# Keys placed into a ring of tile slots, and the probabilities of 18 tiles multiplied on GpSimd

## The chip, the core and the metric

One core of a Trainium2 chip runs the kernel. The metric is the time of one execution in device microseconds. The engines are named as in the profile: PE (TensorE), PEld (its weight loads), DVE (VectorE), ACT (ScalarE), POOL (GpSimd) and SP (SyncE, whose queue issues every DMA here). Each engine works through its own queue in program order and waits on semaphores of the others.

## The reference

Three stages follow one another: a sparse attention, a mixture of eight experts, and a two-layer network with a rational activation. The change touches the first alone.

```
def _attn_ref(q, k, v):                  # 2 batches, 8 heads, 768 positions, 64 wide
    k_sum = k.reshape(B, H, nb, 32, D).max(axis=3)
    v_sum = v.reshape(B, H, nb, 32, D).mean(axis=3)
    scores_l = scale * q @ k.T           # kept where |i - j| < 16, else -1e9
    scores_s = scale * q @ k_sum.T + log(32)
    a = softmax(concatenate([scores_l, scores_s]))
    return a @ concatenate([v, v_sum])
def reference(...):
    x = _attn_ref(...).transpose(0, 2, 1, 3).reshape(1536, 512)
    x = _moe_ref(x, ...)     # logits, 8 rounds of row and column scaling, sum of P[:, e] * relu(x @ w1[e]) @ w2[e]
    return _moe2_ref(x, ...) # g(x @ w_in) @ w_out, g a ratio of polynomials
```

## The kernel before

The attention works on 24 tiles of 64 queries, twelve for each batch. A query tile sees 96 keys (its own 64 and 16 on each side) and 24 block maxima, so its scores have CO = 120 columns for each head; the 8 heads lie in four pairs, which makes a tile of probabilities 128 x 480.

Keys come in three loads of 256 positions for each batch. Of each load the even and odd tokens are copied apart (`by_token`, L399), transposed on PE (`transpose8`, L347) and placed into a tile `kT` of 256 positions (`place`, L359, on ACT, or the second half on DVE). `block_keys` (L375) makes the block maxima `ks` on DVE. `window` (L489) then copies for each tile the 96 keys out of one or two `kT` tiles, and the 24 block maxima, into one of three buffers `kw`; these copies are `pcopy` (L331), that is POOL instructions of line L332.

The loop of L728 sets the order of all engines. Its step s writes the scores of tile s (`scores`, L506: PE, the mask addition L526 and the negated maximum L530 on DVE), the product with the values of tile s-3 (`av`, L558), the transposition of the probabilities of tile s-2 (`trans`, L546), the normalization of tile s-1 (`norm`, L540: an addition L542, a reciprocal L543 and a multiplication L544, all on DVE), the exponentials of tile s (`exps`, L533, ACT) and the window of tile s+2. Then follows what `todo` holds for the step: token copies and placing of later keys and queries, the split of the first expert weights into a high part on POOL (`high_w1`, L135) and a low part on DVE (`low_w1`, L142), the sums of the values and their split (`sum_v`, `means_split`), and the copies of the block means into the three value buffers `vx` (`block_values`, L555, for tiles 0 to 2 of each batch). Between these stand the matmuls of the first expert unit (`mains`, L712), let in by a running credit, and through step 5 short runs of matmuls on the identity (`spin`, L424).

The scores have one PSUM buffer of their own (tag `sc`), so the scores of tile s+1 start only when the mask addition of tile s has read it; the products with the values share one in the same way (tag `xo`); the transposes of keys, queries and probabilities take turns in two (tag `tr`).

Of the kernel before, what the change touches and what calls it, by code (L numbers as in the profile page):

```python
# [10 lines left out]
F32 = mybir.dt.float32  # L11
F32R = mybir.dt.float32r
# [10 lines left out]
def kernel(  # L23
# [285 lines left out]
    with ExitStack() as actx:  # L309
# [1 line left out]
        a1 = actx.enter_context(tc.tile_pool(name="att1", bufs=1, side="right"))  # L311
        psa = actx.enter_context(tc.tile_pool(name="psa", bufs=1, space=PSUM))

        kw = [a1.tile([P, NP, CO], F32, name=f"kw{i}") for i in range(2)]
        kw.append(acc[9][:, 0:NP * CO].rearrange("p (c n) -> p c n", c=NP))
        vx = [a1.tile([CO, DM], F32, name=f"vx{i}") for i in range(3)]
        qs = [a1.tile([P, NP, LT], F32, name=f"qs{i}") for i in range(2)]
        wavg = a1.tile([P, 2 * NB], F32, name="wavg")
        wavgr = a1.tile([P, 2 * NB], F32R, name="wavgr")
        masks = [a1.tile([P, 1, CO], F32, name=f"mask{i}") for i in range(3)]  # L320
        zpad = a1.tile([P, NP, WIN], F32, name="zpad")

        nat = {}
        kT = {}
# [9 lines left out]
        def load_nat(src, nm, b, i):  # L334

            if nm == "q" and b == 0 and i < 2:
                if i:
                    t = spool.tile([P, KC, 2 * P], F32, tag="stg", name="q_0_1")
                else:
                    t = apool.tile([P, NP, LT], F32, tag="kT", name="q_0_0", bufs=4)  # L340
                t = t.rearrange("p c (h t d) -> p (c h) t d", h=2, t=2)
            else:
                t = apool.tile([P, H, 2, D], F32, tag="nat", name=f"{nm}_{b}_{i}", bufs=3)
            nc.sync.dma_start(t, src[b, :, i * LT:(i + 1) * LT, :].rearrange("h (p t) d -> p h t d", t=2))
            nat[nm, b, i] = t
# [12 lines left out]

        def place(dst, par, ps, mul, early=False):  # L359

            o = dst.rearrange("p c (n t) -> p c n t", t=2)[:, :, :, par]
            if par and not early:
                nc.vector.tensor_scalar_mul(o, ps, mul)
            else:
                nc.scalar.mul(o, ps, mul)

        def new_k(b, i):
            kT[b, i] = apool.tile([P, NP, LT], F32, tag="kT", name=f"kT_{b}_{i}", bufs=4)
            if i == 0:
                ks[b] = apool.tile([P, NP, NB], F32, tag="ks", name=f"ks_{b}")  # L370

# [3 lines left out]
        def block_keys(b, i):  # L375
            nb = LT // BLK
            nc.vector.tensor_reduce(
                out=ks[b][:, :, i * nb:(i + 1) * nb],
                in_=kT[b, i].rearrange("p c (n s) -> p c n s", s=BLK),
                axis=AX.X, op=ALU.max,  # L380
            )

        def last_keys(pss):

            nb = LT // BLK
            o = ks[0][:, :, NB - nb:NB]
            m = a1.tile([P, NP, nb], F32, name="odd")
            for dst, ps in zip((o, m), pss):
                nc.vector.tensor_reduce(
                    out=dst, in_=ps.rearrange("p c (n s) -> p c n s", s=BLK // 2), axis=AX.X, op=ALU.max  # L390
                )
            nc.vector.tensor_max(kw[0][:, :, CO - nb:CO], o, m)
            nc.vector.tensor_max(o, o, m)

        qscale = 1.0 / math.sqrt(D)
# [59 lines left out]
        def means_split(i):  # L455
            x = nat.pop(("vsum", 1, i)).rearrange("p h d -> p (h d)")
            if i < 2:
                y = spool.tile([P, KC, 2 * P], F32R, tag="stg", name=f"vhl_{i}").rearrange("p (a b) f -> p a (b f)", a=2)
            else:
                y = apool.tile([P, NP, LT], F32R, tag="kT", name="vhl_2", bufs=4).rearrange("p (a b) f -> p a (b f)", a=2)  # L460
            nc.scalar.copy(y[:, 0], x)
            nc.gpsimd.tensor_sub(y[:, 1], x, y[:, 0].bitcast(F32))
            means[i] = (y[:, 0], y[:, 1])
# [22 lines left out]
                v[b, :, c0:c1, :].rearrange("h p d -> p h d"),  # L486
            )

        def window(t, part=0):  # L489

            b, r = divmod(t, QB)
            w = kw[t % 3]
            i = r // TPL
            e = WIN
            lo, hi = (r % TPL) * QT - e, (r % TPL) * QT + QT + e
            c0, c1 = max(lo, 0), min(hi, LT)
            if part != 2 and lo < 0:
                pcopy(w[:, :, 0:e], kT[b, i - 1][:, :, LT - e:LT] if i else zpad[:, :, 0:e])
            if part != 2:
                pcopy(w[:, :, c0 - lo:c1 - lo], kT[b, i][:, :, c0:c1])  # L500
            if part != 2 and hi > LT:
                pcopy(w[:, :, WK - e:WK], kT[b, i + 1][:, :, 0:e] if i < NL - 1 else zpad[:, :, 0:e])
            if part != 1:
                pcopy(w[:, :, SO:CO], ks[b])

        def scores(t):  # L506
            b, r = divmod(t, QB)
            qt = qT[b, r // TPL]
            ps = psa.tile([P, 2, NP, P], F32, tag="sc", name=f"sc_{t}")
            w = kw[t % 3]  # L510
            i = 0 if r == 0 else (2 if r == QB - 1 else 1)
            m = masks[i]
            o = r % TPL * QT
            for p in range(NP):
                x = p % 2
                p = x * (NP // 2) + p // 2
                for j in range(2):
                    h = slice(j * D, (j + 1) * D)
                    y = (j ^ x) * D
                    nc.tensor.matmul(  # L520
                        ps[y:y + D, x, p % (NP // 2), 0:CO], lhsT=qt[h, p, o:o + QT], rhs=w[h, p, :],
                        start=True, stop=True, tile_position=(j * D, y),
                    )
            a = apool.tile([P, NP, CO], F32, tag="a", name=f"a_{t}", bufs=3)
            sm = apool.tile([P, 4, NP], F32, tag="sm", name=f"sm_{t}", bufs=3)
            nc.vector.tensor_add(  # L526
                a.rearrange("p (x c) n -> p x c n", x=2), ps[:, :, 0:NP // 2, 0:CO],
                m.unsqueeze(1).to_broadcast([P, 2, NP // 2, CO]),
            )
            nc.vector.tensor_reduce(out=sm[:, 0, :], in_=a, axis=AX.X, op=ALU.max, negate=True)  # L530
            st[t] = (a, sm, a)
# [8 lines left out]
        def norm(t):  # L540
            a, sm, _ = st[t]
            nc.vector.tensor_scalar_add(sm[:, 2, :], sm[:, 1, :], 1e-9)  # L542
            nc.vector.reciprocal(sm[:, 3, :], sm[:, 2, :])  # L543
            nc.vector.tensor_mul(a, a, sm[:, 3, :].unsqueeze(2).to_broadcast([P, NP, CO]))  # L544

        def trans(t):  # L546
            a = st.pop(t)[0]
# [57 lines left out]
        make_mask(1)  # L605
        nc.vector.memset(ones, 1.0)
        nc.vector.memset(wavg, 0.0)
        for m in (wavg[:, NB - LT // BLK:NB],):
            nc.gpsimd.memset(m, 1.0 / BLK)
            nc.gpsimd.affine_select(  # L610
                out=m, in_=m, compare_op=ALU.is_ge, fill=0.0, base=0,
                pattern=[[-BLK // 2, LT // BLK]], channel_multiplier=1,
            )
            nc.gpsimd.affine_select(
                out=m, in_=m, compare_op=ALU.is_ge, fill=0.0, base=BLK // 2 - 1,
                pattern=[[BLK // 2, LT // BLK]], channel_multiplier=-1,
            )
        nc.vector.memset(zpad, 0.0)
        nc.scalar.copy(wavgr, wavg)
        for t_ in vx:  # L620
            nc.vector.memset(t_, 0.0)
# [10 lines left out]
        place_k(0, True)  # L632
        by_token("k", 0, 1)
        load_nat(v, "v", 0, 1)
        window(0, 1)
        block_keys(0, 0)
        place_k(1, True)
        by_token("k", 0, 2)
# [10 lines left out]
        block_keys(0, 1)  # L649
        last_keys(pss)  # L650
        by_token("q", 0, 0)
        pcopy(kw[0][:, :, SO:CO - LT // BLK], ks[0][:, :, 0:NB - LT // BLK])
        for par in range(2):
            place(qT[0, 0], par, transpose8("q", 0, 0, par), qscale, True)
        for par in range(2):
            place(kT[0, 2], par, pss[par], 1.0, True)
        window(1)
        spin(2)
        sum_v(0, 0)
        todo = {}  # L660
# [5 lines left out]


        at(0, sum_v, 0, 1)
        at(9, make_mask, 2)
        at(2, block_values, 0)  # L670
        at(2, load_nat, k, "k", 1, 1)
# [56 lines left out]
        for s in range(NQ + AV):  # L728
            if s < NQ:
                scores(s)  # L730
            if s == 2:
                prep_v(0, 0, 1, 2)
            if s == 3:
                prep_q(0, 1)
            if s >= AV:
                av(s - AV)
                if s - AV + 3 < NQ:
                    load_vx(s - AV + 3)
            main(s, 1.5 if s < 12 else 0.9 if s < 22 else 0)
            if 0 <= s - AV + 1 < NQ:  # L740
                trans(s - AV + 1)
                if s < 6:
                    spin(3)
            if 0 < s <= NQ:
                norm(s - 1)
            if s < NQ:
                exps(s)
                if s == 1:
                    sum_v(0, 2)
                if s + 2 < NQ:  # L750
                    window(s + 2)
                if s == 1:
                    by_token("q", 0, 1)
            for f in todo.pop(s, []):
                f()
            if s < 22:
                main(s, 0.8 if s < 12 else 0.4)
            elif s < NQ + AV - 1:
                mains.pop(0)[2]()
# [544 lines left out]
```

## Time and profile before

| | us |
|---|---|
| median of 3 runs | 1370.71 |
| lowest and highest | 1369.95, 1371.71 |
| the profiled execution | 1371.62 |
| its span | 1369.9 |

The span runs from the first to the last recorded instruction; the rest of the profiled execution's time lies around it. The attention's loop fills about the first 115 us; the experts and the last network follow. A timeline row gives the start in us from the span's start, the duration, the engine, the line and the operation with what it writes and reads; a bracket behind it holds the idle time before it and what ended that. A group row gives busy time in us and the mean of one in ns.

### The profile page before, as it was taken

How to read it: one execution, taken by the hardware profiler on the slowest of the kernel's cores; microseconds unless marked ns; L12 is line 12 of the kernel's file. 1: busy time of each engine (PE TensorE's matmuls, PEld its weight loads, DVE VectorE, ACT ScalarE, POOL GpSimd, SP SyncE). 2: the span in 40 equal slices, each digit the busy share in tenths (PEclk: the TensorE clock that was granted, in tenths of full speed). 3: DMA queues.
4: the chain of work that ended last, by engine and by line, in shares of the span. 5: the costliest groups of instructions: out<-in, count | busy, mean ns of one | idle time of the engine just before them, and what ended most of it. 6: DMA issues, size and time to landing. Idle time of an engine off the chain costs nothing.

```text
span 1369.9 us, 20301 instructions
## 1 busy us (share of the span) xinstructions
PE 1348.8 (98%) x7379; PEld 1188.6 (87%) x7379; DVE 1069.5 (78%) x1836; ACT 516.4 (38%) x1156; POOL 826.5 (60%) x1027
## 2 busy tenths in 40 slices
PE   7989999999999999999999999999999999999998
PEld 5768898988999888999889988899888888888887
DVE  6985488777777777777777777777777689998885
ACT  6775412422222222222222222222222379966662
POOL 7864547777777767777777776777777012222221
PEclk9999999999999999999999999999999999999999
DMA  9530011222222222222232222222222421213102
GB/s 273 128 96 12 32 49 58 68 82 71 87 73 74 67 71 67 75 64 82 67 89 76 70 66 74 67 71 72 82 68 69 138 65 47 80 45 93 31 16 77
DMA packets 118883, 102.39 MB, mean 75 GB/s; under 512 B 30080, under 2 KB 99840, under 8 KB 118784
## 3 DMA queue, kind: packets, MB, share of 16 engines
q1 hardware_dynamic: 118784, 101.10, 25.2%
q8 instruction: 58, 0.95, 0.3%
q14 instruction: 41, 0.34, 0.1%
HBM read 81.15 MB, written 19.92 MB: 74 GB/s over the span
## 4 chain that ended last, share of the span: by engine, by line
PE 92%; DVE 4%; ACT 2%; DMA 1%; POOL 1%; issue 1%; SPq 0%; DVEq 0%; ACTq 0%; POOLq 0%
PE p_v L184 12%; PE p_v L185 12%; PE p_v L186 12%; PE p L184 7%; PE p L186 7%; PE p L185 7%; PE X L1087 6%; PE X L1089 6%; PE X L1088 6%; PE Z L1089 3%; PE Z L1088 3%; PE Z L1087 3%; PE Y L1089 2%; PE Y L1088 2%; PE Y L1087 2%; ACT a L536 1%
## 5 line engine op out<-in xcount | busy, mean ns | idle before, releaser
L1199 DVE SCALAR_TENSOR_TENSOR accs<-p_v,Pt,accs 128x512 f32<-128x512 f32 x336 | 244.4, 746 | 90.0 <-PE p_v L186 89.5
L184 PE MATMUL p_v<-w2h_v,hh_v 128*128 128x512 f32 x720 | 283.4, 394 | 0.2
L186 PE MATMUL p_v<-w2h_v,hl_v 128*128 128x512 f32 x720 | 281.7, 391 | 0.0
L185 PE MATMUL p_v<-w2l_v,hh_v 128*128 128x512 f32 x720 | 281.4, 391 | 0.0
L1096 DVE SCALAR_TENSOR_TENSOR hl_v<-s,hh_v 128x384 fp32r<-128x384 f32 x180 | 136.7, 759 | 75.9 <-ACT hh_v L1095 74.6
L234 POOL TENSOR_TENSOR hl<-ta,hh 128x512 fp32r<-128x512 f32 (+1 forms) x52 | 63.2, 1215 | 206.3 <-ACT hh L233 162.0
L1107 ACT COPY s<-X 128x384 f32<-128x384 f32 x56 | 27.0, 482 | 410.2 <-PE X L1089 410.2
L897 POOL TENSOR_SCALAR ce<-ce 128x296 uint32<-128x296 uint32 (+1 forms) x56 | 67.1, 1199 | 180.4 <-DVE ce L888 180.4
L184 PEld LDWEIGHTS p_v<-w2h_v,hh_v 128*128 128x128 f32 x720 | 135.2, 188 | 32.1 <-issue 6.8
L186 PEld LDWEIGHTS p_v<-w2h_v,hl_v 128*128 128x128 f32 x720 | 135.1, 188 | 28.8
L185 PEld LDWEIGHTS p_v<-w2l_v,hh_v 128*128 128x128 f32 x720 | 135.2, 188 | 25.5
L1095 ACT ACTIVATE hh_v<-s 128x384 fp32r<-128x384 f32 x180 | 94.9, 527 | 127.1 <-DVE s L1130 68.7
L110 POOL TENSOR_TENSOR wS<-S,wS 128x256 fp32r<-128x256 f32 x120 | 99.7, 831 | 14.4 <-ACT wS L107 4.7
L184 PE MATMUL p<-xh,w1h 128*128 128x512 f32 (+2 forms) x288 | 103.0, 358 | 0.0
L186 PE MATMUL p<-xh,w1l 128*128 128x512 f32 (+2 forms) x288 | 101.8, 353 | 0.0
L185 PE MATMUL p<-xl,w1h 128*128 128x512 f32 (+2 forms) x288 | 101.7, 353 | 0.0
L184 PE MATMUL p<-w2h,hh 128*128 128x512 f32 (+1 forms) x244 | 94.9, 389 | 0.5 <-DVE accs L262 0.5
L186 PE MATMUL p<-w2h,hl 128*128 128x512 f32 (+1 forms) x244 | 94.4, 387 | 0.1
L185 PE MATMUL p<-w2l,hh 128*128 128x512 f32 (+1 forms) x244 | 94.3, 386 | 0.0
L110 POOL TENSOR_TENSOR w2l_v<-sb,w2h_v 128x512 fp32r<-128x512 f32 x60 | 82.8, 1380 | 5.0
L1089 PE MATMUL X<-th,wS 128*128 128x384 f32 x240 | 80.2, 334 | 0.0
L1088 PE MATMUL X<-tl,wS 128*128 128x384 f32 x240 | 80.2, 334 | 0.0
(226 smaller groups left out, 3351.0 us busy)
## 6 DMA issues: line engine op xcount, KB each, us to landing
sa<-in_moe_w_dram SPq DMA_DIRECT2D x30, 512.0 KB, 3.5
sb<-in_moe_w_dram SPq DMA_DIRECT2D x30, 512.0 KB, 4.4
cv<-in_moe_w_in_dram SPq DMA_DIRECT2D x24, 296.0 KB, 2.9
w1h<-f_in SPq DMA_DIRECT2D x16, 256.0 KB, 2.9
w1l<-f_in SPq DMA_DIRECT2D x16, 256.0 KB, 3.2
w2h<-f_out SPq DMA_DIRECT2D x16, 256.0 KB, 4.4
w2l<-f_out SPq DMA_DIRECT2D x16, 256.0 KB, 4.6
vx<-in_v_dram SPq DMA_DIRECT2D x20, 192.0 KB, 3.3
```

The costliest lines, as they stand in the source:

```text
L110: nc.gpsimd.tensor_sub(lo, src, hi.bitcast(F32))
L184: nc.tensor.matmul(ps, lhsT=sh, rhs=mh, start=(i == 0), stop=False)
L185: nc.tensor.matmul(ps, lhsT=sh, rhs=ml, start=False, stop=False)
L186: nc.tensor.matmul(ps, lhsT=sl, rhs=mh, start=False, stop=(i == n_k - 1))
L234: nc.gpsimd.tensor_sub(hl[:, :n], ta, hh[:, :n].bitcast(F32))
L897: nc.gpsimd.tensor_scalar(out=e, in0=e, scalar1=896, scalar2=0, op0=ALU.subtract, op1=ALU.max)
L1087: nc.tensor.matmul(ps, lhsT=w[:, 0, t], rhs=mh, start=start and t == 0, stop=False, **go)
L1088: nc.tensor.matmul(ps, lhsT=w[:, 0, t], rhs=ml, start=False, stop=False, **go)
L1089: nc.tensor.matmul(ps, lhsT=w[:, 1, t], rhs=mh, start=False, stop=t == 1, **go)
L1095: nc.scalar.activation(hh, src, AF.Relu)
L1096: nc.vector.scalar_tensor_tensor(out=hl, in0=src, scalar=0.0, in1=hh.bitcast(F32), op0=ALU.max, op1=ALU.subtract)
L1199: nc.vector.scalar_tensor_tensor(out=a, in0=ps, scalar=Pt[:, g, e:e + 1], in1=a, op0=ALU.mult, op1=ALU.add)
```

## The change

The three window buffers and the four `kT` tiles become one ring of 16 slots of 120 columns. Keys are placed straight into the middle 64 columns of a tile's slot. POOL then fills only the 16 columns at either edge, for four slots at a time (`halos`, `rest_halos`), and the block maxima, for several slots at a time (`blocks_to`). The multiplication in `norm` goes to POOL for the tiles 3, 5, 7 and 9 to 23; addition and reciprocal stay on DVE. PE gets ten matmuls on the identity before the first transposes. The buffer of the first query load and that of the third split sum (`vhl_2`) move elsewhere.

```
-        kw = [a1.tile([P, NP, CO], F32, name=f"kw{i}") for i in range(2)]
-        kw.append(acc[9][:, 0:NP * CO].rearrange("p (c n) -> p c n", c=NP))
+        NS = 16
+        kw = a1.tile([P, NS, NP, CO], F32, name="kw")
...
-                    t = apool.tile([P, NP, LT], F32, tag="kT", name="q_0_0", bufs=4)
+                    t = kw[:, NS - 3:NS].rearrange("p s c n -> p (s c n)")[:, 0:NP * LT].rearrange("p (c n) -> p c n", c=NP)
...
         def place(dst, par, ps, mul, early=False):
-            o = dst.rearrange("p c (n t) -> p c n t", t=2)[:, :, :, par]
+            if len(dst.shape) == 4:
+                o = dst.rearrange("p s c (n t) -> p s c n t", t=2)[:, :, :, :, par]
+                ps = ps.rearrange("p c (s n) -> p s c n", s=TPL)
+            else:
+                o = dst.rearrange("p c (n t) -> p c n t", t=2)[:, :, :, par]
...
+        def slot(t):
+            return t % NS
+
+        def halos(b, i, first=False):
+            a = slot(b * QB + i * TPL)
+            n = 2 if first else TPL
+            pcopy(kw[:, a:a + n - 1, :, WK - WIN:WK], kw[:, a + 1:a + n, :, WIN:2 * WIN])
+            pcopy(kw[:, a + 1:a + n, :, 0:WIN], kw[:, a:a + n - 1, :, QT:QT + WIN])
+            if i:
+                y = slot(b * QB + i * TPL - 1)
+                pcopy(kw[:, y, :, WK - WIN:WK], kw[:, a, :, WIN:2 * WIN])
+                pcopy(kw[:, a, :, 0:WIN], kw[:, y, :, QT:QT + WIN])
+
+        def rest_halos():
+            a = slot(1)
+            n = TPL - 1
+            pcopy(kw[:, a:a + n - 1, :, WK - WIN:WK], kw[:, a + 1:a + n, :, WIN:2 * WIN])
+            pcopy(kw[:, a + 1:a + n, :, 0:WIN], kw[:, a:a + n - 1, :, QT:QT + WIN])
+
+        def blocks_to(b, r0, r1):
+            a = slot(b * QB + r0)
+            pcopy(kw[:, a:a + r1 - r0, :, SO:CO], ks[b].unsqueeze(1).to_broadcast([P, r1 - r0, NP, NB]))
+
         def new_k(b, i):
-            kT[b, i] = apool.tile([P, NP, LT], F32, tag="kT", name=f"kT_{b}_{i}", bufs=4)
+            a = slot(b * QB + i * TPL)
+            kT[b, i] = kw[:, a:a + TPL, :, WIN:WIN + QT]
...
-        def window(t, part=0):
...
-            w = kw[t % 3]
+            w = kw[:, slot(t)]
...
-            nc.vector.tensor_mul(a, a, sm[:, 3, :].unsqueeze(2).to_broadcast([P, NP, CO]))
+            eng = nc.gpsimd if t >= 9 or t > 2 and t % 2 else nc.vector
+            eng.tensor_mul(a, a, sm[:, 3, :].unsqueeze(2).to_broadcast([P, NP, CO]))
...
+        spin(10)
...
-        window(0, 1)
+        halos(0, 0, True)
...
-        window(1)
+        blocks_to(0, 1, 3)
+        rest_halos()
...
+        at(1, halos, 0, 1)
+        at(2, blocks_to, 0, 3, 6)
+        at(3, halos, 0, 2)
+        at(4, blocks_to, 0, 6, QB)
+        for i in range(NL):
+            at(7 + i, halos, 1, i)
+        at(10, blocks_to, 1, 0, TPL)
+        at(11, blocks_to, 1, TPL, QB)
...
-                if s + 2 < NQ:
-                    window(s + 2)
```

How the instructions stand in the queues shows at two places. The first is POOL in step 4; `k_0` is the first key load of batch 1, `w1h_0` the high part of the first expert weight, `vx` the value buffers. Before:

```order
L332 TENSOR_SCALAR vx_106<-accs 24x512
L332 TENSOR_SCALAR kw_102<-kT_1_192 128x4x96
L332 TENSOR_SCALAR kw_102<-ks_172 128x4x24
L332 TENSOR_SCALAR accs<-k_0_213 128x512 x2
L139 TENSOR_SCALAR w1h_0_457<-s_0_0_217 128x512
```

And with the change, where `a_364` is the tile of probabilities number 3:

```order
L556 TENSOR_TENSOR a_364<-a_364,sm_365 128x480
L331 TENSOR_SCALAR kw<-ks_181 128x24x24
L331 TENSOR_SCALAR accs<-k_0_221 128x512 x2
L139 TENSOR_SCALAR w1h_0_463<-s_0_0_225 128x512
L331 TENSOR_SCALAR accs<-q_2_223 128x512 x2
```

The multiplication of tile 3 and a copy of the block maxima into six slots now stand ahead of the token copies and the weight's high part.

DVE's queue at the same place, from the addition of `norm(3)` on, before:

```order
L542 TENSOR_SCALAR sm_360<-sm_360 128x4
L543 RECIPROCAL sm_360<-sm_360 128x4
L544 TENSOR_TENSOR a_359<-a_359,sm_360 128x480
L145 TENSOR_TENSOR w1l_0_458<-s_0_0_217,w1h_0_457 128x512
L526 TENSOR_TENSOR a_470<-sc_461,mask_112 128x480
```

With the change:

```order
L553 TENSOR_SCALAR sm_365<-sm_365 128x4
L554 RECIPROCAL sm_365<-sm_365 128x4
L145 TENSOR_TENSOR w1l_0_464<-s_0_0_225,w1h_0_463 128x512
L537 TENSOR_TENSOR a_476<-sc_467,mask_111 128x480
L541 TENSOR_REDUCE sm_477<-a_476 128x4
```

The multiplication is gone between the reciprocal and the weight's low part; the rest stands as it did.

The other place is POOL in the steps 14 to 16, around the copies of batch 1's block means into the value buffers. Before:

```order
L332 TENSOR_SCALAR vx_104<-accs 24x512
L332 TENSOR_SCALAR accs<-kT_1_653 128x4x96
L332 TENSOR_SCALAR accs<-ks_508 128x4x24
L332 TENSOR_SCALAR vx_105<-accs 24x512
L332 TENSOR_SCALAR kw_102<-kT_1_653 128x4x96
L332 TENSOR_SCALAR kw_102<-ks_508 128x4x24
L332 TENSOR_SCALAR vx_106<-accs 24x512
```

With the change, where `a_1064`, `a_1130` and `a_1201` are the tiles 13, 14 and 15:

```order
L556 TENSOR_TENSOR a_1064<-a_1064,sm_1065 128x480
L331 TENSOR_SCALAR vx_103<-accs 24x512
L556 TENSOR_TENSOR a_1130<-a_1130,sm_1131 128x480
L331 TENSOR_SCALAR vx_104<-accs 24x512
L556 TENSOR_TENSOR a_1201<-a_1201,sm_1202 128x480
L331 TENSOR_SCALAR vx_105<-accs 24x512
```

Each of the three copies of block means now stands behind the multiplication of a tile.

## Rows read from the trace of the kernel before

**Rows 1.** The page's busy times: us, share of the span, instructions.

```profile
PE 1348.8 (98%) x7379; PEld 1188.6 (87%) x7379; DVE 1069.5 (78%) x1836; ACT 516.4 (38%) x1156; POOL 826.5 (60%) x1027
```

**Rows 2.** Stretches: PE, PEld, DVE, ACT, POOL busy (instructions), clock, DMA share, GB/s.

```profile
20.00:40.00 20.00, 18.83 (x251) 14.71 (x250) 17.12 (x34) 16.04 (x58) 15.56 (x30) 0.99 1.08 284
...
120.00:140.00 20.00, 20.00 (x106) 17.85 (x105) 13.40 (x23) 8.53 (x20) 11.42 (x13) 1.00 0.00 1
```

**Rows 3.** Groups by line and shape, 0 to 125 us: busy us, mean ns.

```profile
L544 DVE TENSOR_TENSOR a<-a,sm 128x480 f32<-128x480 f32 x24 | 19.6, 818 | 0.8
...
L436 POOL TENSOR_TENSOR accs<-v 128x512 f32<-128x512 f32 x6 | 8.1, 1344 | 0.1
...
L332 POOL TENSOR_SCALAR kw<-kT 128x384 f32<-128x384 f32 x8 | 4.9, 612 | 1.2 <-PE sc L520 1.2
L332 POOL TENSOR_SCALAR kw<-ks 128x96 f32<-128x96 f32 x15 | 4.9, 324 | 0.9 <-DVE ks L393 0.9
```

**Rows 4.** Timeline of DVE in step 4.

```profile
28.70 0.18 DVE L543 RECIPROCAL sm<-sm 128x4 f32<-128x4 f32 x1
...
29.49 0.68 DVE L145 TENSOR_TENSOR w1l<-s,w1h 128x512 fp32r<-128x512 f32 x1
30.10 0.65 DVE L526 TENSOR_TENSOR a<-sc,mask 128x480 f32<-128x480 f32 x1
```

**Rows 5.** Timeline of POOL in step 4.

```profile
27.40 0.61 POOL L139 TENSOR_SCALAR w1h<-s 128x512 fp32r<-128x512 f32 x1
```

**Rows 6.** Timeline of PE: trans(4), scores(10), av(7).

```profile
33.66 0.65 PE L550 MATMUL at<-ident,a 128*120 128x128 f32 x4 [0.57 <-ACT kT L365]
...
50.74 0.64 PE L520 MATMUL sc<-kw,qs 64*64 64x120 f32 x16 [0.72 <-POOL w2l L110]
51.72 0.69 PE L567 MATMUL xo<-aT,vx 120*64 120x64 f32 x16 [0.33 <-issue]
```

**Rows 7.** Timeline of PE: av(12), av(13), av(14).

```profile
75.36 0.69 PE L567 MATMUL xo<-aT,vx 120*64 120x64 f32 x16
...
78.90 0.69 PE L567 MATMUL xo<-aT,vx 120*64 120x64 f32 x16 [0.21 <-issue]
...
81.62 0.69 PE L567 MATMUL xo<-aT,vx 120*64 120x64 f32 x16 [0.56 <-DVE sm L542]
```

**Rows 8.** Timeline of DVE: reciprocals of tiles 13, 14, 15 and xl(13).

```profile
74.03 0.18 DVE L543 RECIPROCAL sm<-sm 128x4 f32<-128x4 f32 x1
...
78.67 0.18 DVE L543 RECIPROCAL sm<-sm 128x4 f32<-128x4 f32 x1
...
80.95 0.41 DVE L576 TENSOR_TENSOR xl<-xo,xh 128x256 fp32r<-128x256 f32 x1
...
81.47 0.18 DVE L543 RECIPROCAL sm<-sm 128x4 f32<-128x4 f32 x1
```

**Rows 9.** Timeline of POOL: third value split, block means of tile 12.

```profile
68.09 1.29 POOL L462 TENSOR_TENSOR vhl<-accs,vhl 128x512 fp32r<-128x512 f32 x1 [1.10 <-ACT vhl L461]
...
72.76 0.62 POOL L332 TENSOR_SCALAR vx<-accs 24x512 f32<-24x512 f32 x1
```

**Rows 10.** Stretches of 1 us, columns as in rows 2.

```profile
16.00:17.00 1.00, 0.57 (x16) 0.44 (x16) 0.94 (x2) 1.00 (x6) 0.91 (x2) 1.00 1.21 288
17.00:18.00 1.00, 1.00 (x6) 0.31 (x3) 0.90 (x1) 1.00 (x6) 1.00 (x2) 0.50 1.24 278
```

**Rows 11.** The chain that ended last: start us, us, what.

```profile
3.51 7.10 DMA q<-in_q_dram
...
17.07 4.36 PE vps L446 x6
...
24.28 0.64 PE xo L567 x16
...
25.35 0.42 DVE xl L576
```

**Rows 12.** Waits, 0 to 125 us: total us, times, longest.

```profile
PE at L550 <- DVE a L544: 1.5, 4, 0.7
```

More of the change, by code (lines that the diff above doesn't have):

```diff
@@ L320 @@
         masks = [a1.tile([P, 1, CO], F32, name=f"mask{i}") for i in range(3)]
-        zpad = a1.tile([P, NP, WIN], F32, name="zpad")
         nat = {}
@@ L377, in block_keys @@
             nc.vector.tensor_reduce(
-                out=ks[b][:, :, i * nb:(i + 1) * nb],
-                in_=kT[b, i].rearrange("p c (n s) -> p c n s", s=BLK),
+                out=ks[b][:, :, i * nb:(i + 1) * nb].rearrange("p c (r n) -> p c r n", r=TPL),
+                in_=kT[b, i].rearrange("p r c (n s) -> p c r n s", s=BLK),
                 axis=AX.X, op=ALU.max,
@@ L391, in last_keys @@
                 )
-            nc.vector.tensor_max(kw[0][:, :, CO - nb:CO], o, m)
+            nc.vector.tensor_max(kw[:, 0, :, CO - nb:CO], o, m)
             nc.vector.tensor_max(o, o, m)
@@ L459, in means_split @@
             else:
-                y = apool.tile([P, NP, LT], F32R, tag="kT", name="vhl_2", bufs=4).rearrange("p (a b) f -> p a (b f)", a=2)
+                y = apool.tile([P, 2, DM], F32R, tag="nat", name="vhl_2", bufs=3)
             nc.scalar.copy(y[:, 0], x)
@@ L487, in load_vx @@
             )
-        def window(t, part=0):
-            b, r = divmod(t, QB)
-            w = kw[t % 3]
[L493 to L504, printed above, removed]
         def scores(t):
@@ L509, in scores @@
             ps = psa.tile([P, 2, NP, P], F32, tag="sc", name=f"sc_{t}")
-            w = kw[t % 3]
+            w = kw[:, slot(t)]
             i = 0 if r == 0 else (2 if r == QB - 1 else 1)
@@ L617 @@
             )
-        nc.vector.memset(zpad, 0.0)
+        nc.vector.memset(kw[:, 0, :, 0:WIN], 0.0)
+        nc.vector.memset(kw[:, QB - 1, :, WK - WIN:WK], 0.0)
+        nc.vector.memset(kw[:, slot(QB), :, 0:WIN], 0.0)
         nc.scalar.copy(wavgr, wavg)
@@ L651 @@
         by_token("q", 0, 0)
-        pcopy(kw[0][:, :, SO:CO - LT // BLK], ks[0][:, :, 0:NB - LT // BLK])
+        pcopy(kw[:, 0, :, SO:CO - LT // BLK], ks[0][:, :, 0:NB - LT // BLK])
         for par in range(2):
```

## The prediction

> **What bounds the kernel now.** I read the busy shares first: PE is busy for 98% of the span and no other engine for more than 87% [rows 1]. The stretches by stage then say where PE is not full: at 120 to 140 us it is busy for 20.00 of 20 us, in the attention stage at 20 to 40 us for 18.83, with VectorE (DVE) at 17.12 beside it [rows 2]. All edits lie in the first 115 us, so the reader is to look there only, and a shift of PE at the end of that stage is carried through the full remainder to the end. The edits can win no more than PE's idle time in that stage, and they lose whatever new wait they put in front of PE. PE's order of work is fixed, except for ten small matmuls at the start. I write tile t for one of the 24 tiles of 64 queries and step s for one pass of the loop; step s does scores(s), av(s-3), trans(s-2), norm(s-1), exps(s).
>
> **The window copies and the multiplications.** 18 multiplications leave DVE: 18 x 0.82 = 14.7 us [rows 3]. On GpSimd (POOL) the trace has no 128x480 multiplication. The nearest row is its 128x512 sum of two SBUF tensors, 1.344 us [rows 3]; 480/512 of it is 1.26 us, which I take. The bounds are the 0.82 us that DVE needs and the 1.34 of the longer row. So 18 x 1.26 = 22.7 us come to POOL. The copies that go are one of 0.61 us [rows 3] and one to three smaller ones for each tile; the edge and block copies that come in are fewer and larger. POOL is not relieved, and what decides is when its multiplication stands in front of something that PE or DVE waits for. POOL runs its queue in order, so all that is queued behind a multiplication waits until DVE has made that tile's reciprocal.
> The Trainium skill, GPSIMD Engine Reference, section 3.1 (Elementwise), gives 4497 ns for a 2048-wide POOL sum against 2293 on DVE, and keeps elementwise work on DVE as the rule. By it the multiplication would be 4497 x 480/2048 = 1.05 us, an estimate, and the four that count below would make the sum 0.8 us smaller; the trace's row is longer than that and decides.
>
> **Step 4 (the first place in the order).** Before, POOL did the token copies of k(1,0) and the high part w1h(0) of the first expert weight ahead of time: w1h(0) was done at 28.01 [rows 5]. DVE ended reciprocal(3) at 28.88 and took w1l(0) at 29.49 and the mask addition a(5) at 30.10 [rows 4]. Now POOL's queue is: multiply a(3), block maxima for six slots, two token copies, w1h(0); and w1l(0) on DVE needs w1h(0). From 28.88: 0.1 handover, 1.26, then 576 elements of block maxima (0.7: the 384-wide copy took 0.61, one and a half times that is 0.92), 0.61 for w1h and, at the same width, 2 x 0.61 for the two copies [rows 5], 0.05: 32.8. DVE stands still until then, and a(5), red(5), exps(5), the placing of k(1,0) by ScalarE, and with it trans(4) on PE come 32.8 - 29.5 = 3.3 us later. This trans already waited 0.57 us for that placing [rows 6], so there is no cover: **+3.3**.
> What comes back: after this DVE is no longer behind PE, so the waits of scores(10), 0.72, and of the av behind it, 0.33, go [rows 6]. The first is put down to w2l; but scores(10) cannot start before a(9) is off its PSUM bank, so I read it as DVE's lateness. **-1.05**.
>
> **Steps 9 to 13.** Up to the low part of the third value sum POOL gets three multiplications (3.8 us), four edge copies (at 0.32, the row of a small copy [rows 3], 1.3) and block maxima for twelve slots (two copies, 1152 elements, 1.4 at twice the 0.7 above). It loses four window copies of 0.61 and some eight small ones of 0.32, 5.0, and it had waited 1.10 us for ScalarE there [rows 9]: 3.8 + 1.3 + 1.4 - 5.0 - 1.1 = 0.4. The means on PE wait for it. Between 0 and 1.0; I take **+0.5**.
>
> **SP.** The load of k(1,2) waits for POOL's token copies of k(1,0) and goes out later by what these are late; PE wants it in step 8, itself as late: 0.
>
> **Steps 14 to 17 (the second place).** The block means of batch 1 are copied into the three value buffers on POOL for tiles 12, 13, 14, and av of these tiles waits for them. Before, the first was made at 72.76 to 73.38 [rows 9], well ahead. Now each stands behind a multiplication: a(13), vx(12), a(14), vx(13), a(15), vx(14).
> - av(12): reciprocal(13) ends at 74.03 + 0.18 = 74.21 [rows 8], + 0.05 + 1.26 + 0.05 + 0.62 for the copy [rows 9] = 76.2, against its start at 75.36 [rows 7]: **+0.85**.
> - av(13): reciprocal(14) ends at 78.85 [rows 8], in the same way 80.85, against 78.90 [rows 7]: +1.95.
> - av(14): reciprocal(15) comes after xl(13), and that after av(13). From an av's start to its xl are 25.35 - 24.28 = 1.07 us [rows 11], from xl(13) to the end of reciprocal(15) 81.65 - 80.95 = 0.70 [rows 8]: 80.85 + 1.77 = 82.62, + 1.98 + 0.05 = 84.65, against 81.62 [rows 7]: **+3.0** in all for av(13) and av(14).
> Reciprocals 13 and 14 follow a step of PE's own expert matmuls, so a later PE makes them later too: the terms add up.
>
> **The later tiles.** trans waited 1.5 us in four places for DVE's multiplication [rows 12]. DVE gets there sooner, POOL takes 1.26 for 0.82: from -1.5 to 4 x 0.44 = +1.8; I take **0**.
>
> **The start.** The ten matmuls run on the identity before the first key is there; scores(0) hang on the first q load, which lands 7.10 us after its issue, at 10.61 [rows 11], and this load is the same. The edge copies of the first two slots are as many small POOL copies as before. **0**, covered by that load.
>
> **Sum**: 3.3 - 1.05 + 0.5 + 0.85 + 3.0 = +6.6. The profiled execution took 1371.62 us (its span is 1369.9, the rest lies around it), 0.91 over the median of the three runs, 1370.71. 1371.62 + 6.6 = 1378.2, against the median 1377.3.
>
> **Rivals.**
> - *DVE was the brake (faster).* For it: DVE is busy 17.12 of 20 us at 20 to 40 us [rows 2]. If the new queue order never made anyone wait, PE would lose its waits for DVE: 0.72 + 0.33 [rows 6], 0.56 before av(14) [rows 7], 1.5 before trans [rows 12] = 3.1, so 1370.71 - 3.1 = 1367.6. It decides at reciprocal(3): for w1h(0) to be there at 29.49 it would have to end the 3.9 us of POOL's work earlier, at 25.6, and in the trace it ends at 28.88.
> - *Half of it.* The wait at step 4 is there, but av(12) to av(14) find their block means in time, and trans gains 1.5: 1370.71 + 3.3 - 1.05 - 1.5 = 1371.5. For it: a shorter POOL multiplication; against: 2 us are missing at av(13).
> - *The clock falls.* After a sparse stretch (PE busy for 0.57 of the microsecond from 16 to 17) the granted clock went from 1.00 to 0.50, the 1.2 GHz level [rows 10], and the sums of values took 4.36 us there [rows 11], of which about half, 2.2, is the clock's. The new idle places (about 2 us before each of av(13) and av(14)) look like that stretch: 1377.3 + 2.2 = 1379.5. The Trainium skill, TensorE: Matmul & The Clock Gate, section HAM oscillation, says that idle time between bursts throttles the array again; by that rule this case happens, and the trace shows one such fall.
> - *The change does less than it says*: the order of the instructions shows all 18 multiplications on POOL and the window copies gone, so no chance is kept for that.
>
> **How the numbers follow.** Forecast 0.52, clock 0.10, half 0.20, faster 0.18. The forecast's own ends: with 0.82 for the four multiplications that count 4 x 0.44 less, without the +0.5 and with the -1.5 it is 1373.5; with the upper bounds 1377.3 + 0.3 + 0.5 + 1.8 = 1379.9. The range takes in "half" and part of the clock's case and leaves out the faster one: 1369.0 to 1381.0. A measurement of this kernel can tell about 0.2%, 2.7 us, from no change. Faster 0.18, same 0.20, slower 0.62.
>
> **What would show it.** In the changed profile: a DVE wait of 3 to 4 us before the first w1l for POOL's w1h; trans(4) some 3 us later than 33.66; PE waits before av(12), av(13), av(14) put down to POOL, the latter two about 2 us each; POOL multiplications near 1.26 us; the start of scores(0) unmoved. I am wrong if POOL's multiplication takes under 1 us, if w1l(0) finds its w1h done, or if PE reaches 115 us's work no later than now.

## The result and the profile after

The changed kernel takes 1381.52 us (median of four runs, 1380.61 to 1381.76) against 1370.65 us before (four runs, 1369.95 to 1371.71). The ratio is 1.0077, with a 95% interval of 1.006 to 1.0095: slower by 10.9 us. The prediction was 1377.3 us in a range that ended at 1381.0. The sign was right, the size was 4.2 us short.

The profiled execution of the changed kernel took 1380.61 us, its span is 1378.9: 9.0 us longer than the span before. That is less than 10.9 because the profiled execution is the shortest of the four now and lay near the longest before (1371.62). The page's busy times, to be held against [rows 1]:

```profile
PE 1355.1 (98%) x7399; PEld 1196.1 (87%) x7399; DVE 1055.8 (77%) x1820; ACT 516.9 (37%) x1156; POOL 826.5 (60%) x1013
```

VectorE lost 13.7 us of work. POOL, which got the 18 multiplications and lost the window copies, has exactly the busy time that it had. TensorE (PE) is busy 6.3 us longer. Its 20 additional records are the ten new matmuls on the identity, and they alone take 4.64 us, ahead of the first transposes:

```profile
1.43 4.64 PE L457 MATMUL spin<-ident 128*128 128x128 f32 x20 [1.43 <-POOL ident masks.py:199]
```

They delay nothing, as scores(0) starts at 13.19 us against 13.28 before. (Ten of the same matmuls take 2.40 us in an experiment below; why they take twice as long here, at a granted clock of 1.00 in the profile, is open.) Of the first 12 us PE is busy for 9.18 against 5.69; from there to the end it is busy 2.7 us longer and idle 6.3 us longer. The 2.7 us need an explanation too, since none of PE's real work was changed.

The waits of PE from 0 to 125 us (total us, times, longest) say where it stands now:

```profile
PE xo L579 <- POOL vx L331: 3.8, 3, 2.1
PE sc L531 <- DVE a L537: 3.1, 3, 1.6
PE at L562 <- POOL a L556: 1.6, 3, 0.7
PE at L562 <- ACT kw L368: 1.6, 1, 1.6
```

The first line is av(12), av(13), av(14), which wait for POOL's block means; the fourth, and the longest wait of the second, are step 4. Two pieces of PE's timeline (start us, us, operation) show both places. First scores(6), trans(4), scores(7) and trans(5):

```profile
33.22 0.64 PE L531 MATMUL sc<-kw,qs 64*64 64x120 f32 x16 [1.61 <-DVE a L537]
...
36.07 1.11 PE L562 MATMUL at<-ident,a 128*120 128x128 f32 x4 [1.60 <-ACT kw L368]
...
39.02 1.08 PE L531 MATMUL sc<-kw,qs 64*64 64x120 f32 x16
...
42.90 0.60 PE L562 MATMUL at<-ident,a 128*120 128x128 f32 x4
```

Then av(12), av(13), trans(14), av(14) and trans(15), against [rows 7]:

```profile
80.02 0.69 PE L579 MATMUL xo<-aT,vx 120*64 120x64 f32 x16 [0.62 <-POOL vx L331]
...
85.41 0.69 PE L579 MATMUL xo<-aT,vx 120*64 120x64 f32 x16 [2.07 <-POOL vx L331]
86.03 1.09 PE L562 MATMUL at<-ident,a 128*120 128x128 f32 x4
...
89.18 1.12 PE L579 MATMUL xo<-aT,vx 120*64 120x64 f32 x16 [1.06 <-POOL vx L331]
...
94.32 0.60 PE L562 MATMUL at<-ident,a 128*120 128x128 f32 x4
```

The reader is to see two things here. The brackets are the predicted waits. The durations were not predicted: trans takes 1.11 and 1.09 us where it took 0.65 [rows 6], and scores(7) 1.08 where [rows 6] have 0.64 for scores(10). Stretches of the same trace, with columns as in [rows 2], give the reason:

```profile
36.00:41.00 5.00, 4.93 (x44) 3.92 (x44) 4.09 (x9) 3.91 (x14) 3.21 (x5) 0.50 0.53 144
41.00:86.00 45.00, 39.85 (x486) 32.99 (x482) 32.85 (x67) 30.53 (x110) 31.94 (x47) 0.99 0.46 120
86.00:92.00 6.00, 4.94 (x44) 3.80 (x41) 2.67 (x8) 2.85 (x11) 2.97 (x4) 0.51 0.26 64
```

The granted clock is 0.50, the 1.2 GHz level, from 36 to 41 and about 0.5 from 86 to 92 us. Stretches of 1 us show where each fall begins:

```profile
34.00:35.00 1.00, 0.47 (x16) 0.33 (x12) 0.93 (x4) 1.00 (x6) 0.23 (x1) 0.94 1.03 275
35.00:36.00 1.00, 0.00 (x0) 0.00 (x0) 1.00 (x3) 1.00 (x6) 0.00 (x0) 0.50 0.41 107
...
85.00:86.00 1.00, 0.59 (x16) 0.55 (x16) 0.00 (x0) 0.00 (x0) 0.36 (x1) 1.00 0.98 377
86.00:87.00 1.00, 1.00 (x8) 0.68 (x4) 0.45 (x2) 0.37 (x1) 0.00 (x0) 0.54 0.16 59
```

The first begins behind the wait of 1.61 us and within that of 1.60, the second behind the wait of 2.07; the wait of 1.06 lies inside the second fall. Before, scores(7) and trans(5) stood here, at the full clock:

```profile
35.69 0.64 PE L520 MATMUL sc<-kw,qs 64*64 64x120 f32 x16
...
38.41 0.65 PE L550 MATMUL at<-ident,a 128*120 128x128 f32 x4
```

From the start of trans(4) to that of trans(5) it is 38.41 - 33.66 = 4.75 us before and 42.90 - 36.07 = 6.83 now: 2.08 for the first fall. From av(13) to trans(15) it is 8.91 us now, of which 1.06 is the wait of av(14); what the clock costs there was taken from the experiment below that removes it.

The cause of the first place is on VectorE and POOL. POOL's queue in step 4 (multiplication of tile 3, block maxima, two token copies, w1h(0)), then VectorE's w1l(0):

```profile
28.10 0.99 POOL L556 TENSOR_TENSOR a<-a,sm 128x480 f32<-128x480 f32 x1 [3.11 <-DVE sm L554]
29.06 0.67 POOL L331 TENSOR_SCALAR kw<-ks 128x576 f32<-128x576 f32 x1
29.69 1.20 POOL L331 TENSOR_SCALAR accs<-k 128x512 f32<-128x512 f32 x2
30.86 0.62 POOL L139 TENSOR_SCALAR w1h<-s 128x512 fp32r<-128x512 f32 x1
```

```profile
31.51 1.08 DVE L145 TENSOR_TENSOR w1l<-s,w1h 128x512 fp32r<-128x512 f32 x1 [3.58 <-POOL w1h L139]
```

POOL stood idle for 3.11 us with all of this queued behind a multiplication whose operand was not there; w1h(0), done at 28.01 before [rows 5], is done at 31.48.

### The profile page after: what moved, and what is told of

Its sections match the earlier page's. It is cut to its first block, busy times and chain, and to the rows that moved or that the text cites. A ratio compares the mean times of both kernels' runs of the same rounds, so it can differ in the third digit from the quotient of the medians.

```text
span 1378.9 us, 20343 instructions
## 1 busy us (share of the span) xinstructions
PE 1355.1 (98%) x7399; PEld 1196.1 (87%) x7399; DVE 1055.8 (77%) x1820; ACT 516.9 (37%) x1156; POOL 826.5 (60%) x1013
## 4 chain that ended last, share of the span: by engine, by line
PE 92%; DVE 2%; DMA 2%; ACT 2%; POOL 1%; issue 1%; SPq 0%; POOLq 0%; ACTq 0%
PE p_v L184 12%; PE p_v L185 12%; PE p_v L186 12%; PE p L184 8%; PE p L186 7%; PE p L185 7%; PE X L1109 6%; PE X L1111 6%; PE X L1110 6%; PE Z L1110 3%; PE Z L1111 3%; PE Z L1109 3%; PE Y L1111 2%; PE Y L1110 2%; PE Y L1109 2%; PE xo L579 1%
```

## Experiments

The theory after the result: two places where urgent work stands behind a multiplication in POOL's queue, and at each a fall of PE's clock set off by the idle time. The rivals: the falls have another cause or cost nothing; POOL's slower multiplication hurts at every tile; the ring itself costs something.

**One multiplication back.** `eng = nc.gpsimd if t >= 9 or t in (5, 7) else nc.vector`, the rest as changed: tile 3 on VectorE.

> The changed kernel with one multiplication, that of tile 3, back on DVE. Theory (a queue wait and the clock fall that it sets off): in the changed kernel trans(4) starts at 36.07 us, 2.41 later than before although scores(3) starts 0.83 earlier, so POOL's late w1h(0) costs 3.24; and from 36 to 41 us the granted clock is 0.50, over which the work from trans(4) to trans(5) takes 6.83 us instead of 4.75, 2.08 more. Both go; the 1.05 that scores(10) and av(7) give back today are then not given back. 1381.5 - 3.24 - 2.08 + 1.05 = 1377.2, the DVE wait of 3.58 us for w1h is gone and the clock stays at 1.00 from 36 to 41. Rival A (the wait only; the clock falls for another reason): 1381.5 - 3.24 + 1.05 = 1379.3, with 0.50 still granted. Rival B (the slower POOL multiplication costs a little in every tile): one tile of 18 changes nothing to speak of, 1381.0 to 1381.5.

Measured: 1375.13 us (six runs, 1373.24 to 1377.02), 6.4 less. VectorE's wait of 3.58 us for w1h and the first clock fall are gone. Moving one tile of 18 back takes away more than half of the loss, so it is not a small cost in each tile. It came out lower than the theory's 1377.2 for a reason that was not foreseen. The waits of av(12) to av(14) are still there (4.6 us in three places), but in the profiled run the clock did not fall at them:

```profile
82.00:83.00 1.00, 0.00 (x0) 0.00 (x0) 0.84 (x3) 1.00 (x6) 0.81 (x1) 1.00 0.81 184
83.00:84.00 1.00, 0.07 (x2) 0.07 (x4) 0.48 (x1) 0.62 (x4) 0.83 (x3) 1.00 0.10 20
84.00:85.00 1.00, 1.00 (x18) 0.89 (x19) 0.00 (x0) 0.34 (x1) 0.95 (x1) 1.00 0.00 0
```

The two slowest of the six runs have a mean granted clock of 0.996, the others 0.999 to 1.000. The mean over a whole run doesn't say where the clock fell, but by it the same waits are followed by a fall in some executions and not in others.

**Block means one step earlier.** `at(1 + t, block_values, t)` for tiles 12 to 14, in place of `at(2 + t, ...)`: each copy is queued ahead of the next tile's multiplication.

> The changed kernel with the three copies of block means for tiles 12, 13 and 14 issued one step earlier, so that each stands in POOL's queue ahead of the next tile's multiplication. Theory: the three PE waits of av(12), av(13) and av(14) for POOL (0.62, 2.07 and 1.06 us, 3.75 in all) go, and with them the clock fall from 86 to 92 us, over which the work from av(13) to trans(15) takes 8.91 us instead of 6.19, of which 1.06 is the wait and 1.66 the clock: 1381.5 - 3.75 - 1.66 = 1376.1. Rival A (waits only, the clock falls anyway): 1377.8. Rival B (the copies are not what av waits for, or what comes next is as late): over 1380.

Measured: 1375.15 us (1373.96 to 1376.26), 6.4 less. No av waits for POOL any more and the second fall is gone; the first place is as it was, with waits of 1.6 and 1.6 us and a fall from 35 to 42 us.

**Both.**

> Both edits: tile 3's multiplication on DVE, and the three copies of block means one step earlier. Theory: the two places are independent and add up: 1381.5 - 4.3 - 5.4 = 1371.8, about the kernel before, with no clock fall between 30 and 115 us. Rival A (waits only): 1381.5 - 2.2 - 3.75 = 1375.5. Rival B (something else of the change is slow): over 1376, and PE's starts stay late against before at places without a POOL wait.

Measured: 1371.12 us (ten runs, 1369.77 to 1372.08), a ratio to before of 1.000 (0.9991 to 1.001). The two places together are the whole loss; the clock is 1.00 from 30 to 92 us. They don't simply add up: each edit alone gains 6.4 us, 12.8 in sum, and both together 10.4. The difference of 2.4 is about the 2.1 by which the first edit had come out under its theory: the fall at the second place, which most of its runs did not have.

**The ring alone**, all 24 multiplications on VectorE.

> The ring alone: all 24 multiplications on DVE, the rest of the changed kernel as it is. Theory (all the loss comes from multiplications that stand in POOL's queue): neither of the two places waits, 1371.8 less the 1.6 us that trans waits today for POOL's multiplication, plus up to 1.5 that it waited before for DVE's: 1370.2 to 1372. Rival (the ring costs something itself, its edge copies or the later loads of values): over 1374 with waits of scores for POOL's edge copies.

Measured: 1372.01 us (ten runs, 1369.2 to 1377.02), ratio 1.0011 (1.000 to 1.0022). What the ring costs lies between nothing and 0.2%, at the limit of what these runs can tell. Its profiled run, 1374.36, is one of the slower ones and shows an accident of its own, av(9) waiting for its values from DRAM, and the clock falling behind that wait:

```profile
64.25 0.81 PE L579 MATMUL xo<-aT,vx 120*64 120x64 f32 x16 [1.83 <-DMA vx<-in_v_dram]
```

**The multiplications alone**: the kernel before, window copies kept, with the 18 multiplications on POOL.

> The kernel before with only the 18 multiplications moved to POOL and the window copies kept (no ring). Theory (a multiplication hurts by what stands behind it in POOL's queue, and the ring takes work out of that queue): at step 4 the queue holds the multiplication of tile 3 and, behind it, the window copies of tile 6 and the token copies and w1h(0), so w1l(0) is late by some 3 us, and av(12) to av(14) wait as in the changed kernel; the window copies now stand behind a multiplication too, and scores(t) need them, so more waits come: slower than the changed kernel, 1384 to 1392. Rival A (the ring gains nothing and costs nothing): 1380 to 1383. Rival B (it is the ring's edge copies that make the loss): under 1376.

Measured: 1382.30 us (1380.77 to 1383.52), ratio 1.0083 (1.0069 to 1.0097). My theory that the window copies would make it worse fell; rival A holds. The same two places show, with a larger second one and the clock falling at both (35 to 40, 80 to 84 and 87 to 94 us), and the wait of scores for POOL's copies is only 0.4 us:

```profile
PE xo L568 <- POOL vx L332: 5.7, 3, 2.2
PE sc L520 <- DVE a L526: 4.0, 4, 1.5
...
PE sc L520 <- POOL kw L332: 0.4, 1, 0.4
```

So the multiplications alone cost about what the whole change costs, 0.8%, and the ring alone at most 0.2%.

**Only the order in POOL's queue.** All multiplications stay on POOL; token copies and w1h(0) go ahead of tile 3's: `W1 = [(3, 4), ...]`, and `at(3 if t == 5 else t - 1, by_token, ...)`.

> The changed kernel with all its multiplications on POOL, and only the order in POOL's queue changed at step 4: the two token copies of k(1,0) and the high part w1h(0) stand ahead of the multiplication of tile 3 instead of behind it. Theory (what hurts is the place in the queue, not the multiplication): w1h(0) is done near 27.9 us as before, VectorE doesn't wait for it, and the kernel loses as much as with tile 3's multiplication on VectorE: 1375.1, or up to 0.6 more since trans(3) then waits for POOL. Rival (a 1.0 us multiplication on POOL in place of 0.66 to 0.82 on VectorE makes tile 3 late whatever stands behind it): 1380 or more.

Measured: 1377.08 us (1374.59 to 1377.82), 4.4 less. POOL's w1h(0) is done at 27.90, its multiplication follows at 29.44, and VectorE takes w1l(0) right behind its reciprocal:

```profile
26.88 1.02 POOL L139 TENSOR_SCALAR w1h<-s 128x512 fp32r<-128x512 f32 x1
29.44 1.29 POOL L556 TENSOR_TENSOR a<-a,sm 128x480 f32<-128x480 f32 x1 [1.54 <-DVE sm L554]
```

```profile
29.21 0.68 DVE L145 TENSOR_TENSOR w1l<-s,w1h 128x512 fp32r<-128x512 f32 x1
```

PE's waits before scores(6) and trans(4) and the first clock fall are gone, so the step-4 wait was the place in the queue, not the multiplication. The 2.0 us more than with tile 3 on VectorE are beyond the 0.6 that I had allowed: trans(3) waits 0.74 us for POOL, and three of these four runs have a mean clock of 0.996, the profiled one among them with a fall from 82 to 89 us, which the kernel with tile 3 on VectorE had, by the mean clock, in two of its six runs.

**The clock by itself.** Small matmuls on the identity, whose results nobody uses, in front of PE's four long waits.

> The changed kernel with small matmuls on the identity put in front of PE's four long waits (10 before scores(6), 10 before trans(4), 13 before av(13), 6 before av(14), about 0.14 us each, so 1.4, 1.4, 1.9 and 0.9 us); no result uses them. They take no wait away, they only keep PE at work while it would wait. Theory (idle PE lets the clock fall): the clock stays at 1.00 through 36 to 41 and 86 to 92 us, and the 2.08 + 1.66 us that the work there takes longer go: 1381.5 - 3.7 = 1377.8, which is also the price of the waits by themselves (6.6 over before). Rival A (the clock falls for another reason): still 0.50 there, 1381.5 or a little more. Rival B (the clock costs nothing since the waits behind it absorb it): clock at 1.00 and still 1381.

Measured: 1380.72 us (1380.39 to 1380.89). The clock stays up at both places, as the theory says, yet only 0.8 us is gained. I had mis-sized the filling:

```profile
32.10 2.40 PE L457 MATMUL spin<-ident 128*128 128x128 f32 x20
```

Ten matmuls are 20 records and take 2.40 us, not 1.4, longer than the wait that they stood in; they pushed PE back by what the clock gave. So this run left open what the clock costs, and it was done again with fewer:

```
spin(6) before scores(6) and before trans(4); spin(8) before av(13), spin(4) before av(14)
```

> The changed kernel with filling matmuls again, fewer of them: one measured 0.24 us (20 records in 2.40 us), not 0.14, so that the earlier ones (2.40, 2.50, 3.17 and 1.60 us) were longer than the waits that they stood in (1.61, 1.60, 2.07 and 1.06) and used up what the clock gave back. Now 6, 6, 8 and 4: 1.44, 1.44, 1.92 and 0.96 us. Theory: clock at 1.00 from 36 to 41 and from 86 to 92 us and nothing pushed: 1381.5 - 2.08 - 1.66 = 1377.8, up to 1.7 more where the clock falls at 17 us instead. Rival (the clock's price is small, the waits are the whole loss): 1380 to 1381 with the clock at 1.00.

Measured: 1378.15 us (1377.49 to 1378.26), 3.4 less than the changed kernel, with every wait for data left in place. The two stretches now have the full clock:

```profile
36.00:41.00 5.00, 4.70 (x59) 3.73 (x58) 4.90 (x10) 4.89 (x17) 2.50 (x4) 1.00 0.58 154
...
86.00:92.00 6.00, 5.15 (x51) 4.19 (x44) 2.27 (x8) 2.39 (x11) 4.35 (x6) 1.00 0.29 66
```

and the starts of trans(4), trans(5), av(13), av(14) and trans(15) are:

```profile
36.79 0.65 PE L562 MATMUL at<-ident,a 128*120 128x128 f32 x4
...
41.55 0.60 PE L562 MATMUL at<-ident,a 128*120 128x128 f32 x4
...
84.47 0.69 PE L579 MATMUL xo<-aT,vx 120*64 120x64 f32 x16
...
88.24 0.69 PE L579 MATMUL xo<-aT,vx 120*64 120x64 f32 x16 [0.85 <-POOL vx L331]
...
91.71 0.60 PE L562 MATMUL at<-ident,a 128*120 128x128 f32 x4
```

41.55 - 36.79 = 4.76 us, the 4.75 of before, where the changed kernel needs 6.83; 91.71 - 84.47 = 7.24 against 8.91. The clock cost 2.07 + 1.67 = 3.7 us, and it was the idle PE that let it fall, since only its idle time was filled. The two profiled executions are only 2.4 us apart (spans of 1378.9 and 1376.5), in the main because this one has a clock fall near 17 us as well, as the kernel before has [rows 10] and the changed kernel's doesn't.

**Towards a better kernel.** Three steps on top of both mended places. First the multiplications of tiles 14, 20 and 22 back on VectorE, where trans waited for POOL; then `halos(0, 1)` and `blocks_to(0, 3, 6)` ahead of `by_token("q", 0, 1)` in POOL's queue; then `spin(3)` before scores(1) and scores(2), in PE's two waits of 0.94 us.

> The kernel with both places mended (tile 3's multiplication on DVE, block means one step earlier), and besides the multiplications of tiles 14, 20 and 22 on DVE, where trans waits 0.48, 0.71 and 0.71 us for POOL. Theory (trans takes the slower multiplication where DVE would be in time): before, the same three places waited 0.25 us each for DVE, so 0.23 + 0.46 + 0.46 = 1.15 us: 1371.1 - 1.15 = 1370.0. Rival (DVE is late there again and the gain is lost, or later waits absorb it): 1371.1.

> The same with the edge copies of tiles 4 to 7 and the block maxima of tiles 3 to 5 put ahead of the two token copies of q(0,1) in POOL's queue: scores(3) waits 1.17 us for them, while POOL itself stands 0.99 us waiting for that q load. Theory: scores(3) no longer waits for POOL, PE is about 1.1 us earlier from there to the next wait, and the wait of av(3) for its values, 0.87 us, takes part of it: 0.2 to 1.1 us less than without, 1369 to 1369.8. Rival (the values' load sets av(3) and takes all of it): the same as without, 1370.0.

> The best kernel so far (1369.9: tiles 3, 14, 20 and 22 on VectorE, block means a step earlier, edge copies first) with 3 filling matmuls, 0.72 us, in each of the two waits of 0.94 us before scores(1) and scores(2). In its profile the clock falls to 0.50 from 17 to 20.5 us, and the sums of values took 4.45 us there against 2.76 where it does not fall. Theory (a fuller PE before 17 us keeps the clock up): the sums take 2.76 us in every run; of the 1.69 some is taken by the wait of scores(3) for its edge copies and of av(3) for its values, so 0.5 to 1.2 less than without: 1368.7 to 1369.4, and a narrower spread. Rival A (later waits absorb all of it): 1369.9. Rival B (the fall comes all the same, or the matmuls push scores back): 1369.9 to 1370.5.

Measured, eleven runs each: 1370.30, 1369.90 and 1369.31 us; ratios to before of 0.9994 (0.9985 to 1.0003), the same again, and 0.9991 (0.9982 to 1.000). The steps were expected to give 1370.0, 1369 to 1369.8 and 1368.7 to 1369.4; the runs come near that, but no step is clear of the spread of the one before. In the third, PE is fuller before 17 us and the sums of values run at the full clock. Two stretches of the second of these kernels, without the filling, and its sums of values, which took 4.36 us in the kernel before [rows 11]:

```profile
14.00:17.00 3.00, 1.31 (x33) 0.99 (x34) 2.58 (x5) 1.77 (x10) 1.97 (x3) 1.00 1.22 290
17.00:20.00 3.00, 3.00 (x4) 0.51 (x4) 2.90 (x5) 1.53 (x8) 3.00 (x7) 0.53 1.22 274
```

```profile
16.90 4.45 PE L474 MATMUL vps<-accs,wavg 128*24 128x512 f32 x6
```

and the same of the third, with the filling:

```profile
14.00:17.00 3.00, 2.86 (x45) 2.22 (x45) 2.59 (x5) 1.78 (x10) 2.06 (x3) 1.00 1.21 290
17.00:20.00 3.00, 3.00 (x10) 0.85 (x10) 2.90 (x6) 1.83 (x9) 3.00 (x7) 1.00 1.22 289
```

```profile
16.90 2.75 PE L474 MATMUL vps<-accs,wavg 128*24 128x512 f32 x6
```

Of the 1.70 us won there 1.32 go into a new wait of av(3) for its values. A last kernel put that load ahead of the expert weight that stood before it on SP (`at(3, dma_w, 0, 2, 0, 6)` for `at(2, ...)`):

> The kernel with the filling matmuls before scores(1) and scores(2) (1369.3), with one more exchange, on SP: the load of tile 3's values stands ahead of the load of an expert weight that waits for PE's trans(1), instead of behind it. In the trace without the exchange the value load is issued at 24.21 us and lands 7.1 us later, and av(3) waits 1.3 us for it. Theory (the order of issue on SP sets it): it can be issued once av(0) is done, near 23.1, so it lands 1.1 us earlier and av(3) waits 0.2: 1368.2 to 1368.8. Rival (the DMA engines, at a busy share of 0.9 or more in these microseconds, deliver it no earlier, or the weight is late in its place): 1369.3 or more.

Measured: 1369.32 us (eleven runs, 1368.27 to 1372.21), ratio to the kernel before beside it 0.9997 (0.9988 to 1.0006): no gain. av(3) no longer waits, but av(4) does, for the next load:

```profile
30.54 0.69 PE L579 MATMUL xo<-aT,vx 120*64 120x64 f32 x16
...
35.45 0.69 PE L579 MATMUL xo<-aT,vx 120*64 120x64 f32 x16 [0.91 <-DMA vx<-in_v_dram]
```

The DMA engines have a busy share of 1.10 from 24 to 36 us there, and the exchange of two loads moved the wait by a tile. The best kernel is 1.6 us under the one before as timed beside it (1369.31 against 1370.88); the interval of its ratio reaches 1.000, so it is not shown to be faster.

## Why the prediction was wrong in size

Point by point, by its own terms. The kernel with the fitted filling (1378.15 us; span of its profiled execution 1376.5) is the one to compare with, since in it the waits stand alone, without the two falls, and its profile has a fall near 17 us like that of before; shifts are PE's starts against before.

- **Step 4, +3.3.** trans(4) moved by 36.79 - 33.66 = 3.13, and scores(3) had stood 0.13 ahead: 3.26. Right. Two errors cancelled in it. The multiplication took less than assumed (below), and w1l(0), while POOL copied beside it, took 1.08 us instead of 0.68 [rows 4].
- **Given back, -1.05.** scores(10) and av(7) took back 0.96. Right, and so was reading that wait as VectorE's lateness.
- **Steps 9 to 13, +0.5.** Nothing of it came in the way that was forecast: the means did not wait. Some 1.0 us appeared in the same stretch for other reasons, about half of it a wait of av(9) for its values (0.64; 0.78 in the changed kernel), the rest at scores(13) and av(10). Not predicted, so that the term came out near its size by luck. In the other kernels that wait of av(9) for its values is between nothing and 1.83 us; what sets it is open.
- **av(12), +0.85**: 0.70. **av(13) and av(14), +3.0**: 1.87 + 1.05 = 2.92. Right, and so is the mechanism: each waits for its block means behind a multiplication.
- **Later trans, 0**: trans(19) no longer waits (-0.82), trans(20) and trans(22) wait 0.71 each for POOL, where they waited 0.25 for VectorE; with what scores(20) adds it is +0.45 in sum, inside the bounds.
- **The start, 0**: scores(0) at 13.19 in the changed kernel against 13.28. Right. The profile of before holds a clock fall at 17 us that the changed kernel's does not, and trans(0) starts 1.76 us earlier there; scores(3) then waits 0.87 us for POOL's edge copies and block maxima, which the prediction had put at nothing, so 0.83 of the 1.76 is left.
- **POOL's multiplication, 1.26 us**: wrong, and the row chosen for it was the wrong one.

```profile
L556 POOL TENSOR_TENSOR a<-a,sm 128x480 f32<-128x480 f32 x18 | 18.1, 1003 | 30.6 <-DVE sm L554 29.3 <-ACT aT L564 0.9 <-PE vps L499 0.4
```

It takes 1.00 us on average. The prediction had also worked out an estimate of 1.05 us from the 4497 ns that the Trainium skill, GPSIMD Engine Reference, section 3.1 (Elementwise), gives for a 2048-wide sum; the trace agrees with that rather than with the 1.26 scaled from the longer sum.

The prediction's sum was +6.6, and the kernel without the two falls has a span 6.6 us longer than before; as timed it is 7.3 us over the kernel before beside it. Along the way PE's last product with values starts 7.06 us later (121.48 against 114.42): the points above, less the 0.13 that PE was ahead and 0.18 won between trans(4) and trans(7). What takes back the rest behind it was not traced. That the sum is met so closely is in part luck, with the two errors that cancel at step 4 and the 1.0 us in steps 9 to 13 that has another cause. **The step that failed is the rival "The clock falls"**: it was given one chance in ten, one fall and 2.2 us, as an alternative to the forecast, so that the forecast's sum had the clock at nothing. In the runs of the changed kernel it belonged into the sum: the falls came at both places and cost 2.07 and 1.67 us, and all four timed runs have the same mean clock of 0.995. 1378.15 + 3.7 = 1381.9, against the 1381.52 measured. The prediction looked for a fall only before av(13) and av(14) and not at step 4, although its own term there put 3.3 us of idle time into PE within a few microseconds, about as much as the 1.95 + 1.05 at the second place; and the trace of before showed [rows 10] what follows a sparse PE.

The Trainium skill, TensorE: Matmul & The Clock Gate, section HAM oscillation, says that idle time between bursts throttles the array again. The runs agree in kind: filling the waits kept the clock at 1.00. The waits in that section's case are longer than those forecast here, though, so that "by that rule this case happens" read more into it than it says. The runs differ from it in two things: waits of 1.61 and 1.60 us, and one of 2.07 us, were enough here, and one and the same wait is not always followed by a fall.

## What to carry to other kernels

Before an operation is moved to an engine that works as a helper, list what stands behind it in that engine's queue and who waits for each item: here one multiplication of 18, in front of a weight split, and three in front of 0.62 us copies made the whole loss, waits and clock together, and moving the copies one step ahead undid their part at no cost that the runs show. When a forecast puts idle time of some microseconds into a stretch that already has short gaps, price the work behind it at the lower clock in the sum or as a case with a good chance, not as a remote one; the same waits were followed by a fall in most runs here, not in all. And where a wait can't be removed at once, filling it with work that nobody needs shows how much of a loss is the wait and how much the clock, provided the filling is shorter than the wait.

## What was not expected of the hardware

- The same waits of PE before av(12) and av(13) (about 0.6 and 2.1 us) were followed by a fall of the clock in one profile and not in another. By the mean clock of the runs, a fall came in all four of the changed kernel, in three of four with only the order of the copies changed, and in two of six with tile 3 on VectorE. In the profiled run of that last kernel PE also waited 1.93 us before av(14), and the granted clock stayed at 1.00. What decides it is open.
- With the ring alone, ten runs lie between 1369.2 and 1377.0 us. Those with a mean clock of 1.00 reach from 1369.2 to 1371.7, the three with 0.997 from 1373.7 to 1377.0: so most of the spread goes with the falls.
- VectorE's 128x512 subtraction took 1.08 us instead of 0.68 while POOL copied, and two POOL copies took 1.63 instead of 1.20 beside it. The kernel before has both lengths as well (0.68 and 1.09; 1.20 and 1.60). Whether the two engines slow each other was not tested by itself.
